# Softmax attention beside a spectral filter: ten score tiles to VectorE and GpSimd, squares to VectorE, a step budget carried from step to step

## The chip, the cores and the metric

The kernel runs on one NeuronCore of a Trainium2 chip. The metric is the device time of one execution in microseconds; less is better. The engines are named as in the profile: PE (TensorE matmuls) and PEld (its weight loads), DVE (VectorE), ACT (ScalarE), POOL (GpSimd), SP (SyncE, which only issues transfers here).

## What is computed

Two branches read the same input `x` (2048 tokens, 448 features) and are mixed per token by a gate.

```python
def reference(A_x, A_wqkv, A_wo, B_x, B_w_r, B_w_i, gate_w):
    # H = 16 heads of Dh = 28, S = 2048, D = 448, all bfloat16
    x = A_x
    g = sigmoid((x * gate_w).sum(-1, keepdims=True))
    q, k, v = split_heads(x @ wqkv)                 # each (1, 16, 2048, 28)
    p = softmax(einsum("bhqd,bhkd->bhqk", q, k) * Dh ** -0.5)
    a = merge_heads(einsum("bhqk,bhkd->bhqd", p, v)) @ wo
    X = rfft2(B_x as float32) * (w_r + 1j * w_i)    # (1, 2048, 225)
    b = irfft2(X, s=(S, D)).astype(bfloat16)
    return g * a + (1 - g) * b
```

## The kernel before

**Attention.** Scores stand transposed: keys on the 128 partitions, queries along the columns. The 16 heads form four groups T of four heads (28 features padded to 32 rows each, so that four heads share the 128 rows), and the 2048 queries form four blocks q of 512. A pair (T, q) is a *chunk*; there are 16. A chunk has 16 key blocks i times 4 heads s, that is 64 *tiles* of 128 x 512 scores, 1024 tiles in all. The tiles, in order, are cut into *steps* of three, 342 steps, so a chunk is 21.33 steps (`SPAN`) and some steps hold tiles of two chunks.

A step m works like this. `scores(m)` makes three matmuls into one three-bank PSUM tile `psS` (two such tiles take turns). `exps(m)` is one ScalarE instruction, `Pt`, which applies exp with the scale to all 1536 columns and writes bfloat16. `values` takes finished tiles in groups of eight (`GROUP`) and makes the value matmuls into `psPV`; a constant one in each head's value block gives the softmax sums in the same matmuls. A constant feature row of the keys, `kb`, and the negated half norms of queries and keys, which `q_units` and `k_units` compute, bound the exponent, so that no maximum over the scores is needed. When a chunk's 64 value matmuls are done, `normalise` transposes `psPV` on VectorE (`turned`, tile `oU`), one step later takes the reciprocal and multiplies on GpSimd (`scaled`, tiles `rc` and `on`), and three steps later transposes back on VectorE (`back`, into `oT`, which is the place of `qT`).

**Background work.** Everything else is cut into *units*: generators that yield the model cost of the next matmul and then issue it. They are the projections (`q_units`, `k_units`, `v_unit`, `first_values`), the spectral branch as matmuls with Fourier matrices (`f1_units`, `stage_A_units`, `f34_units`, `f678_units`), and the output tiles (`out_tile`). All of them use one PSUM bank, `ps_bg`, with one buffer, which VectorE empties at the end of a unit. The spectral weights are multiplied in `f34_units` with half of the products on VectorE and half on GpSimd (tiles `cm_t`, `G`).

`plan` gives each unit a due step; units are kept sorted by it. In each step, after the value matmuls, `other_work` issues pieces of the current unit while the next piece's model cost fits the step's room; when a unit ends, the step's background work ends too. If `scores` needs a projection that is not yet made, `need` runs units without regard to the room until it is. The queries of a chunk c, where T is above 0 or q is above 0, are due from step 21.33 c - 13 to 21.33 c - 8. `filler` adds matmuls on a zero tile, `warm`, ahead of the scores where the model's PE activity of the last steps falls short of a target.

The model's numbers (`ROOM` = 1.22 us for a step's PE work, `SWITCH` = 0.11 us for a change of kind, `MM` = 1/2400 us for a column) set only the order and number of the instructions. Each engine works in the order of the program (`keep_in_program_order`), so whatever stands behind a waiting instruction on its engine waits with it.

**Around it.** `head` runs before step 0: transposes of x, the keys of group 0 and its first query block. `gate`, called in the unit at step 8, computes the gate on ScalarE and VectorE, and `w_copy` copies projection weights on GpSimd. `finish` does the last chunk's normalisation and output.

Of the kernel before, what the change touches and what calls it, by code (L numbers as in the profile page):

```python
# [9 lines left out]
BF16 = mybir.dt.bfloat16  # L10
# [5 lines left out]
P = 128  # L16
# [10 lines left out]
NQ = S // QW  # L27
SCALE = float(DH) ** -0.5
ROOM = 1.22
SWITCH = 0.11  # L30
GROUP = 8
PTB = 6
# [2 lines left out]
FEND = 318  # L35
BUSY = 1650
UNIT = 1000
F = D // 2 + 1
F2 = 2 * F
J = P // NT  # L40
# [94 lines left out]
class Kernel:  # L135
    def __init__(self, tc, A_x, A_wqkv, A_wo, B_w_r, B_w_i, gate_w, out):
        self.tc = tc
        self.nc = Engines(tc)
        self.A_x, self.A_wqkv, self.A_wo = A_x, A_wqkv, A_wo
        self.B_w_r, self.B_w_i, self.gate_w = B_w_r, B_w_i, gate_w  # L140
        assert tuple(A_x.shape) == (1, S, D)
        self.x = A_x[0].rearrange("(p t) d -> p t d", t=NT)
        self.outv = out[0].rearrange("(p t) d -> p t d", t=NT)
        self.units = []
        self.activity = [800, 800]
        self.current = None
        self.later = {}

    def setup_pools(self, ctx):
        tc = self.tc  # L150
# [26 lines left out]
    def loads(self):  # L177
# [13 lines left out]
        self.xtok = [per.tile([P, 4, D], BF16, name=f"xtok{g}", tag=f"xb{g}") for g in range(4)]  # L191
        for g in range(4):
            nc.sync.dma_start(out=self.xtok[g][:], in_=self.x[:, 4 * g:4 * g + 4, :])
        self.kbt = per.tile([P, 1], F32, name="kbt")
        self.kb = self.kbt[:, 0:1]
        wv = self.A_wqkv[:, 2 * D:3 * D].rearrange("(c p) n -> p c n", p=CK)
# [17 lines left out]
        self.wq = self.Wqk[:, :, 0:D].rearrange("p c (h d) -> p c h d", d=DH)  # L214
        self.xT = per.tile([CK, NC_, S], BF16, name="xT")
        self.qT = [per.tile([P, S], BF16, name=f"qT{T}") for T in range(NTH)]
        self.kT = [per.tile([P, S], BF16, name=f"kT{T}") for T in range(NTH)]
        self.oT = self.qT
        self.nm = [per.tile([P, NQ], F32, name=f"nm{T}") for T in range(NTH)]
        self.nhk = [per.tile([P, 1], F32, name=f"nhk{T}") for T in range(NTH)]  # L220
# [139 lines left out]
    def q_units(self, T, g):  # L360
        nc = self.nc
        st = {}

        def a():
            pq = self.ps_bg([P, QW], F32, name="pq")
            yield from self.proj_mm(pq[:], self.WqP, T, g)
            qr = st["qr"] = self.rot3.tile([P, QW], BF16, name="qr")
            nc.vector.tensor_copy(out=qr[:], in_=pq[:])
            sq = st["sq"] = self.rot3.tile([P, QW], BF16, name="sq")
            nc.gpsimd.tensor_tensor(out=sq[:], in0=qr[:], in1=qr[:], op=ALU.mult)  # L370

        def b():
            pq = self.ps_bg([P, QW], F32, name="pq2")
            yield QW * MM
            nc.tensor.matmul(pq[:], lhsT=self.sel, rhs=st["sq"][:], start=True, stop=True)
            nc.vector.scalar_tensor_tensor(out=self.qT[T][:, QW * g:QW * g + QW], in0=pq[:],
                                           scalar=self.nhk[T][:, 0:1], in1=st["qr"][:],
                                           op0=ALU.add, op1=ALU.add)
        return (("qa", T, g), a), (("q", T, g), b)

    def k_units(self, T, g):
        nc = self.nc
        st = {}

        def a():
            pk = self.ps_bg([P, QW], F32, name="pkb")
            yield from self.proj_mm(pk[:], self.WkP, T, g)
            kT = self.kT[T][:, QW * g:QW * g + QW]
            nc.vector.tensor_scalar(out=kT, in0=pk[:], scalar1=self.kb, scalar2=None,
                                    op0=ALU.add)  # L390
            sq = st["sq"] = self.rot3.tile([P, QW], BF16, name="sq")
            nc.gpsimd.tensor_tensor(out=sq[:], in0=kT, in1=kT, op=ALU.mult)

        def b():
            pn = self.ps_bg([P, QW], F32, name="pn")
            yield QW * MM
            nc.tensor.matmul(pn[:], lhsT=self.sel, rhs=st["sq"][:], start=True, stop=True)
            nc.vector.tensor_reduce(out=self.nm[T][:, g:g + 1], in_=pn[:], axis=AX.X, op=ALU.min)
# [98 lines left out]
        return fill  # L497

    def other_work(self, m, room, base=0):
        done = base  # L500
        while self.current is None and self.units and self.units[0][0] <= m:
            self.next_unit()
            self.left = UNIT
        while room > 0 and self.current is not None:
            key, g, cost = self.current
            if cost > room:
                break
            room -= cost
            done += cost / MM
            self.left = max(self.left - cost / MM, cost / MM)  # L510
            try:
                self.current = (key, g, g.send(None))
            except StopIteration:
                self.finished(key)
                break
        self.activity.append(done)

    def need(self, key):
        while key not in self.done:
# [22 lines left out]
    def gate(self):  # L542
# [5 lines left out]
        nc.vector.tensor_scalar(out=self.omg[:], in0=self.gsb[:], scalar1=-1.0, scalar2=1.0,  # L548
                                op0=ALU.mult, op1=ALU.add)

    def attention(self):
        nc = self.nc
        chunks = [(T, q) for T in range(NTH) for q in range(NQ)]
        seq = [(ci, i, s) for ci in range(len(chunks)) for i in range(NT) for s in range(4)]
        steps = [seq[m:m + 3] for m in range(0, len(seq), 3)]
        n = len(steps)
        psS, Pt = {}, {}

        group = [len([1 for k in range(3 * m, 3 * m + 3) if k % GROUP == GROUP - 1])
                 for m in range(n + 1)]  # L560

        def scores(m):
            T, q = chunks[steps[m][-1][0]]
# [8 lines left out]
            for e, (ci, i, s) in enumerate(steps[m]):  # L572
# [12 lines left out]
        self.psPV = None  # L585
        pending = []

        def values(m, least):
            room = 0.0
            while len(pending) >= least:  # L590
                ci = pending[0][2][0]
                T, q = chunks[ci]
                for pt, e, (_, i, s) in pending[:least]:
                    self.need(("v", 1, i) if T else ("v", 0, i // 2))
                    if i == 0 and s == 0:
                        self.psPV = self.ps_pv([P, QW], F32, name="psPV")
                    nc.tensor.matmul(self.psPV[32 * s:32 * s + 32, :],
                                     lhsT=self.vsb[:, i, 4 * T + s, :], rhs=pt[:, e, :],
                                     start=(i == 0), stop=(i == NT - 1), tile_position=(0, 32 * s))
# [3 lines left out]
                if i == NT - 1 and s == 3:  # L603
                    self.normalise(m, T, q, self.psPV)
            return room

        scores(0)
        for m in range(n + 1):
            if m < n:
                exps(m)  # L610
            if m + 1 < n:
                scores(m + 1)
            if m > 0:
                pending += [(Pt[m - 1], e, x) for e, x in enumerate(steps[m - 1])]
# [51 lines left out]
    def normalise(self, m, T, q, psPV):  # L666
# [8 lines left out]
        def scaled():  # L675
# [5 lines left out]
            def back():  # L681
# [239 lines left out]
```

## Time and profile before

| What | Value |
|---|---|
| Median of 3 runs | 501.36 us (499.49, 501.36, 501.70) |
| Profiled execution | 500.02 us, of which the span of its instructions is 498.2 us |
| Mean granted TensorE clock | 0.984 of full speed |
| PE | 407.1 us busy, 82% of the span, 3152 matmuls |
| ACT | 471.6 us busy, 95%, 364 instructions |
| DVE | 195.4 us busy, 39%, 338 instructions |
| POOL | 85.6 us busy, 17%, 125 instructions |
| Steps | the first exponential starts at 17.93 us, the last at 489.2 us |

How to read it: a row of the costliest groups names line, engine, operation, written tile <- read tiles, partitions x elements and type, the count, then the group's busy time, the mean length of one instruction, and the idle time of that engine just before instructions of the group with what ended it. Here nearly all instructions are recorded by one helper, so the line is always L118 and the tiles' names tell them apart. Neighbouring instructions of one engine overlap, so busy time divided by the count is less than the mean length. A timeline row has start, duration, engine, group, count and, in brackets, the idle time before with its releaser.

### The profile page before, as it was taken

The numbers are of one execution on the slowest core, as the hardware profiler recorded it, in microseconds if no ns is written. First come the engines' busy times: TensorE is split into PE (matmuls) and PEld (weight loads), VectorE is DVE, ScalarE is ACT, GpSimd is POOL, SyncE is SP. The second block draws the span as 40 slices with busy tenths as digits, with TensorE's granted clock in tenths as the row PEclk, the third lists the DMA queues.
The fourth block names the chain that finished last, engine by engine and source line by source line (L and its number), as shares of the span: only waits on it lengthen the run. The fifth ranks groups of instructions, "written<-read, shape, count | busy, mean of one in ns | idle before, by whom it ended". The sixth has DMA issues, their size and how long they took to land.

```text
span 498.2 us, 7735 instructions
## 1 busy us (share of the span) xinstructions
PE 407.1 (82%) x3152; PEld 151.9 (30%) x3154; DVE 195.4 (39%) x338; ACT 471.6 (95%) x364; POOL 85.6 (17%) x125
## 2 busy tenths in 40 slices
PE   9777787888888888887887788888888888887886
PEld 5322222222322223323333332332333333322221
DVE  5321222232322325326676773424444333322325
ACT  5899989999999999999989999997999999997993
POOL 4100201040000110003455551001000000000000
PEclk9999989899999999999979999999999999999999
DMA  8700000000000000000122210000000001100002
GB/s 257 184 1 1 2 1 0 1 0 1 2 0 1 0 1 1 0 2 19 42 53 61 52 35 1 1 1 0 22 21 22 22 1 30 51 9 21 18 11 65
DMA packets 15515, 12.67 MB, mean 25 GB/s; under 512 B 6984, under 2 KB 14600, under 8 KB 15480
## 3 DMA queue, kind: packets, MB, share of 16 engines
q1 hardware_dynamic: 14728, 11.91, 8.8%
q8 instruction: 24, 0.39, 0.3%
q10 hardware_dynamic: 752, 0.28, 0.2%
q14 instruction: 11, 0.09, 0.1%
HBM read 10.35 MB, written 1.84 MB: 24 GB/s over the span
## 4 chain that ended last, share of the span: by engine, by line
ACT 54%; issue 20%; PE 17%; DVE 8%; POOL 1%; DVEq 0%; ACTq 0%; POOLq 0%
ACT Pt L118 54%; PE psS L118 5%; PE psPV L118 3%; PE pq L118 2%; PE pvp L118 1%; DVE qT L118 1%; DVE cm_t L118 1%; DVE Xri L118 1%; DVE qr L118 1%; PE psB L118 1%; PE pw L118 1%; PE pt L118 1%; PE pk L118 1%; POOL sq L118 1%; DVE nm L118 1%
## 5 line engine op out<-in xcount | busy, mean ns | idle before, releaser
L118 ACT ACTIVATE Pt<-psS 128x1536 bf16<-128x1536 f32 x342 | 460.2, 1659 | 13.0 <-PE psS L118 12.9
L118 PE MATMUL psS<-qT,kT 32*128 32x512 bf16 x1024 | 136.5, 387 | 31.1 <-ACT Pt L118 22.7
L118 PEld LDWEIGHTS <-kT 32*128 32x128 bf16 x1024 | 47.8, 91 | 148.6 <-issue 140.4
L118 PE MATMUL psPV<-Pt,vsb 128*32 128x512 bf16 x1024 | 80.4, 389 | 0.0
L118 PE MATMUL psS<-warm 128*128 128x512 bf16 (+15 forms) x152 | 43.3, 329 | 23.7 <-ACT Pt L118 20.2
L118 POOL TENSOR_TENSOR sq<-qr 128x512 bf16<-128x512 bf16 x16 | 16.6, 1040 | 162.1 <-DVE qr L118 162.1
L118 POOL TENSOR_TENSOR on<-oU,rc 128x512 bf16<-128x512 f32 x15 | 15.7, 1048 | 101.3 <-DVE rc L118 101.3
L118 POOL TENSOR_TENSOR sq<-kT 128x512 bf16<-128x512 bf16 x12 | 12.5, 1040 | 90.7 <-DVE kT L118 90.7
L118 PEld LDWEIGHTS <-warm 128*128 128x128 bf16 x178 | 17.7, 101 | 27.1 <-issue 23.3
L118 PEld LDWEIGHTS <-vsb 128*32 128x32 bf16 x1024 | 15.6, 94 | 30.0 <-issue 30.0
L118 POOL TENSOR_TENSOR cm_t<-Xri,Wg 128x225 bf16<-128x225 bf16 x32 | 20.2, 654 | 23.1 <-DVE Xri L118 22.9
L118 DVE CAST X<-psx 128x450 bf16<-128x450 f32 x16 | 10.0, 626 | 33.1 <-PE psx L118 33.1
L118 DVE CAST qr<-pq 128x512 bf16<-128x512 f32 x16 | 11.1, 691 | 28.3 <-PE pq L118 28.3
L118 DVE CAST vsb<-pvp 128x336 bf16<-128x336 f32 x16 | 8.1, 508 | 34.6 <-PE pvp L118 34.6
L118 PEld LDWEIGHTS <-xT 112*128 112x128 bf16 x192 | 14.1, 97 | 24.7 <-issue 20.8
L118 DVE TENSOR_SCALAR bm<-psY,omg 128x448 bf16<-128x448 f32 x16 | 10.9, 683 | 27.2 <-PE psY L118 27.2
L118 PE MATMUL pq<-xT,WqP 112*128 112x512 bf16 x64 | 18.9, 382 | 1.3 <-DVE ZT L118 0.3
L118 DVE TENSOR_SCALAR kT<-pkb,kbt 128x512 bf16<-128x512 f32 x12 | 9.0, 751 | 25.5 <-PE pkb L118 25.5
L118 DVE CAST V<-psA 113x512 bf16<-113x512 f32 x16 | 11.1, 691 | 19.7 <-PE psA L118 19.7
L118 DVE CAST U<-psA 113x512 bf16<-113x512 f32 x16 | 11.1, 692 | 19.2 <-PE psA L118 19.1
L118 PE MATMUL psx<-Bd,xT 112*128 112x450 bf16 x64 | 17.0, 356 | 1.7 <-DVE X L118 0.6
L118 PE MATMUL psY<-Binv,ZT 113*128 113x448 bf16 x64 | 16.7, 355 | 1.8 <-DVE fin L118 0.5
(82 smaller groups left out, 359.2 us busy)
## 6 DMA issues: line engine op xcount, KB each, us to landing
RBg<-cRB SPq DMA_DIRECT2D x16, 128.0 KB, 2.1
xtok<-in_A_x_dram SPq DMA_DIRECT2D x4, 448.0 KB, 4.4
out_dram<-fin SPq DMA_DIRECT2D x15, 112.0 KB, 1.7
CSg<-cCS SPq DMA_DIRECT2D x16, 96.0 KB, 1.9
Wg<-in_B_w_r_dram SPq DMA_DIRECT2D x16, 56.2 KB, 1.8
Wg<-in_B_w_i_dram SPq DMA_DIRECT2D x16, 56.2 KB, 1.9
Wqk<-in_A_wqkv_dram SPq DMA_DIRECT2D x1, 784.0 KB, 10.3
Binv<-cBinv SPq DMA_DIRECT2D x1, 448.0 KB, 13.7
```

The costliest lines, as they stand in the source:

```text
L118: return lambda *a, **k: self._tc.keep_in_program_order(f(*a, **k))
```

## The change

Four things are done together.

1. In chunks 0 to 6 and 10 to 12 (`AWAY`), tile i = 0 of head s = 0 is taken out of the ScalarE sequence. It is computed in the chunk's third step, as the third tile of that step's `psS`; the exponential of that step covers two tiles. VectorE multiplies the third tile by scale / ln 2 into float32 (`sx`), and GpSimd raises 2 to that power, elementwise, into bfloat16 (`px`). Its value matmul enters the queue 14 steps later (`LAG`). The start and stop flags of the value matmuls go by a count for each head, and `back` comes 14 steps after the normalisation instead of 3 for head groups 0 to 2.
2. The squares in `q_units` and `k_units` move from GpSimd, where they read the bfloat16 copy twice, to VectorE, where one operand is the PSUM bank and the other the copy.
3. A step's background work may exceed `ROOM` by `ALLOW` = 0.25 us of model time; what it exceeds (`over`) is taken from the steps that follow.
4. The four key tiles `kT` share two buffers, allocated when a group's first key unit runs.

```diff
+ALLOW = 0.25
+LOG2 = SCALE / float(np.log(2.0))
+AWAY = {c: [2] for c in list(range(7)) + [10, 11, 12]}
+LAG = 14
...
+        self.two = per.tile([P, 1], F32, name="two")
+        nc.vector.memset(self.two[:], 2.0)
...
-        self.kT = [per.tile([P, S], BF16, name=f"kT{T}") for T in range(NTH)]
+        self.kT = {}
+        self.new_keys(0)
...
             sq = st["sq"] = self.rot3.tile([P, QW], BF16, name="sq")
-            nc.gpsimd.tensor_tensor(out=sq[:], in0=qr[:], in1=qr[:], op=ALU.mult)
+            nc.vector.scalar_tensor_tensor(out=sq[:], in0=pq[:], scalar=0.0, in1=qr[:],
+                                           op0=ALU.add, op1=ALU.mult)
...
+    def new_keys(self, T):
+        self.kT[T] = self.per.tile([P, S], BF16, name=f"kT{T}", tag=f"kT{T % 2}")
...
-            nc.gpsimd.tensor_tensor(out=sq[:], in0=kT, in1=kT, op=ALU.mult)
+            nc.vector.scalar_tensor_tensor(out=sq[:], in0=pk[:], scalar=self.kb, in1=kT,
+                                           op0=ALU.add, op1=ALU.mult)
...
     def other_work(self, m, room, base=0):
-        done = base
+        done, start = base, room
...
+        return start - room
...
+    def steps(self, chunks):
+        away, acts = {}, []
+        for ci in range(len(chunks)):
+            away[ci] = [(o, (ci, 4 * k, k)) for k, o in enumerate(AWAY.get(ci, []))]
+            out = [x for _, x in away[ci]]
+            acts += [(ci, i, s) for i in range(NT) for s in range(4) if (ci, i, s) not in out]
+        steps, first = [], {}
+        while acts:
+            ci = acts[0][0]
+            m = len(steps)
+            first.setdefault(ci, m)
+            off = [away[ci].pop(0)[1]] if away[ci] and away[ci][0][0] <= m - first[ci] else []
+            k = 3 - len(off)
+            steps.append((acts[:k], off))
+            del acts[:k]
+        return steps
...
             if m > 1:
-                pv = GROUP // 4 * QW * group[m - 2]
-                room = ROOM - 3 * SWITCH - QW * MM - pv * MM
+                pv = GROUP // 4 * QW * group[m - 1]
+                room = ROOM + ALLOW - self.over - 3 * SWITCH - QW * MM - pv * MM
                 self.base += self.filler(m - 1, room, QW + pv, ps)
...
         def exps(m):
-            ne = len(steps[m])
-            pt = Pt[m] = self.rotP.tile([P, 3, QW], BF16, name="Pt")
-            nc.scalar.activation(out=pt[:, 0:ne, :], in_=psS.pop(m)[:, 0:ne, :], func=ACT.Exp,
+            acts, away = steps[m]
+            ne = len(acts)
+            ps = psS.pop(m)
+            pt = self.rotP.tile([P, 3, QW], BF16, name="Pt")
+            nc.scalar.activation(out=pt[:, 0:ne, :], in_=ps[:, 0:ne, :], func=ACT.Exp,
                                  scale=SCALE)
+            ready.setdefault(m + 1, []).extend((pt[:, e, :], x) for e, x in enumerate(acts))
+            for x in away:
+                sx = self.rot2.tile([P, QW], F32, name="sx")
+                nc.vector.tensor_scalar(out=sx[:], in0=ps[:, ne, :], scalar1=LOG2, scalar2=None,
+                                        op0=ALU.mult)
+                px = self.rot2.tile([P, QW], BF16, name="px")
+                nc.gpsimd.tensor_tensor(out=px[:], in0=bcast_last(self.two[:, 0:1], QW),
+                                        in1=sx[:], op=ALU.pow)
+                ready.setdefault(m + LAG, []).append((px[:], x))
...
-                                     start=(i == 0), stop=(i == NT - 1), tile_position=(0, 32 * s))
+                                     start=(count[s] == 0), stop=(count[s] == NT - 1),
+                                     tile_position=(0, 32 * s))
+                    count[s] += 1
...
             fill = self.base - QW
             used = fill * MM + values(m, 4 if late else GROUP)
+            used += 2 * SWITCH + QW * MM
             if m < n:
-                self.other_work(m, ROOM - SWITCH - QW * MM - used - SWITCH, self.base)
+                used += self.other_work(m, ROOM + ALLOW - self.over - used, self.base)
+            self.over = max(0.0, self.over + used - ROOM)
...
-            self.later.setdefault(m + 3, []).append(back)
+            self.later.setdefault(m + (3 if T == NTH - 1 else LAG), []).append(back)
```

More of the change, by code (lines that the diff above doesn't have):

```diff
@@ L147, in __init__ @@
         self.later = {}
+        self.over = 0.0
     def setup_pools(self, ctx):
@@ L385, in a @@
         def a():
+            if g == 0:
+                self.new_keys(T)
             pk = self.ps_bg([P, QW], F32, name="pkb")
@@ L549, in gate @@
                                 op0=ALU.mult, op1=ALU.add)
+    def steps(self, chunks):
[13 more added lines that the diff above has]
+            del acts[:k]
+        assert not any(away.values())
+        return steps
     def attention(self):
@@ L553, in attention @@
         chunks = [(T, q) for T in range(NTH) for q in range(NQ)]
-        seq = [(ci, i, s) for ci in range(len(chunks)) for i in range(NT) for s in range(4)]
-        steps = [seq[m:m + 3] for m in range(0, len(seq), 3)]
+        steps = self.steps(chunks)
         n = len(steps)
-        psS, Pt = {}, {}
-        group = [len([1 for k in range(3 * m, 3 * m + 3) if k % GROUP == GROUP - 1])
-                 for m in range(n + 1)]
+        psS, ready = {}, {}
+        ends = [0]
+        for m in range(n + 1):
+            new = len(steps[m - 1][0]) if m else 0
+            new += sum(1 for k in (m - LAG,) if k >= 0 and steps[k][1])
+            ends.append(ends[-1] + new)
+        group = [ends[m + 1] // GROUP - ends[m] // GROUP for m in range(n + 1)]
         def scores(m):
-            T, q = chunks[steps[m][-1][0]]
+            tiles = steps[m][0] + steps[m][1]
+            T, q = chunks[tiles[len(steps[m][0]) - 1][0]]
             self.need(("k", T, NQ - 1))
@@ L568, in scores @@
             if m > 1:
-                pv = GROUP // 4 * QW * group[m - 2]
-                room = ROOM - 3 * SWITCH - QW * MM - pv * MM
+                pv = GROUP // 4 * QW * group[m - 1]
+                room = ROOM + ALLOW - self.over - 3 * SWITCH - QW * MM - pv * MM
                 self.base += self.filler(m - 1, room, QW + pv, ps)
-            for e, (ci, i, s) in enumerate(steps[m]):
+            for e, (ci, i, s) in enumerate(tiles):
                 T, q = chunks[ci]
@@ L579, in exps @@
         def exps(m):
-            ne = len(steps[m])
-            pt = Pt[m] = self.rotP.tile([P, 3, QW], BF16, name="Pt")
-            nc.scalar.activation(out=pt[:, 0:ne, :], in_=psS.pop(m)[:, 0:ne, :], func=ACT.Exp,
-                                 scale=SCALE)
+            acts, away = steps[m]
[3 more added lines that the diff above has]
+            nc.scalar.activation(out=pt[:, 0:ne, :], in_=ps[:, 0:ne, :], func=ACT.Exp,
+                                 scale=SCALE)
+            ready.setdefault(m + 1, []).extend((pt[:, e, :], x) for e, x in enumerate(acts))
[7 more added lines that the diff above has]
+                ready.setdefault(m + LAG, []).append((px[:], x))
         self.psPV = None
         pending = []
+        count = [0] * 4
         def values(m, least):
@@ L590, in values @@
             while len(pending) >= least:
-                ci = pending[0][2][0]
-                T, q = chunks[ci]
-                for pt, e, (_, i, s) in pending[:least]:
+                for ap, (ci, i, s) in pending[:least]:
+                    T, q = chunks[ci]
                     self.need(("v", 1, i) if T else ("v", 0, i // 2))
-                    if i == 0 and s == 0:
+                    if not any(count):
                         self.psPV = self.ps_pv([P, QW], F32, name="psPV")
                     nc.tensor.matmul(self.psPV[32 * s:32 * s + 32, :],
-                                     lhsT=self.vsb[:, i, 4 * T + s, :], rhs=pt[:, e, :],
-                                     start=(i == 0), stop=(i == NT - 1), tile_position=(0, 32 * s))
+                                     lhsT=self.vsb[:, i, 4 * T + s, :], rhs=ap,
+                                     start=(count[s] == 0), stop=(count[s] == NT - 1),
+                                     tile_position=(0, 32 * s))
+                    count[s] += 1
                 del pending[:least]
@@ L602, in values @@
                 self.base += least // 4 * QW
-                if i == NT - 1 and s == 3:
+                if min(count) == NT:
+                    count[:] = [0] * 4
                     self.normalise(m, T, q, self.psPV)
@@ L612, in attention @@
                 scores(m + 1)
-            if m > 0:
-                pending += [(Pt[m - 1], e, x) for e, x in enumerate(steps[m - 1])]
+            pending += ready.pop(m, [])
             late = m >= n - 3
```

## The prediction

> **What bounds the kernel now.** I read the page first (engines, slices, costliest groups), then the groups with shapes kept apart, ScalarE's timeline, the stretches table, and last PE, VectorE and GpSimd around the places where ScalarE sits idle. The groups with shapes apart give the bound and the prices:
>
> ```profile
> L118 ACT ACTIVATE Pt<-psS 128x1536 bf16<-128x1536 f32 x341 | 459.7, 1661 | 13.0 <-PE psS L118 12.9
> L118 ACT ACTIVATE Pt<-psS 128x512 bf16<-128x512 f32 x1 | 0.8, 841 | 0.0
> L118 DVE SCALAR_TENSOR_TENSOR qT<-pq,nhk,qr 128x512 bf16<-128x512 f32 x15 | 11.2, 749 | 11.3 <-PE pq L118 11.3
> L118 POOL TENSOR_TENSOR on<-oU,rc 128x512 bf16<-128x512 f32 x15 | 15.7, 1048 | 101.3 <-DVE rc L118 101.3
> L118 POOL TENSOR_TENSOR sq<-qr 128x512 bf16<-128x512 bf16 x16 | 16.6, 1040 | 162.1 <-DVE qr L118 162.1
> L118 POOL TENSOR_TENSOR sq<-kT 128x512 bf16<-128x512 bf16 x12 | 12.5, 1040 | 90.7 <-DVE kT L118 90.7
> ```
>
> The exponentials fill 459.7 of the 498.2 us span, one every 459.7/341 = 1.348 us (neighbours overlap, so one lasts 1661 ns). All ScalarE loses between them is 13.0 us, and PE ends nearly all of it. ScalarE's timeline from 103 us on (start, duration, group, count, idle before) shows where:
>
> ```profile
> 104.94 145.19 ACT L118 ACTIVATE Pt<-psS 128x1536 bf16<-128x1536 f32 x108 [0.19 <-PE psS L118]
> ...
> 264.01 75.33 ACT L118 ACTIVATE Pt<-psS 128x1536 bf16<-128x1536 f32 x56 [0.62 <-PE psS L118]
> 342.47 115.63 ACT L118 ACTIVATE Pt<-psS 128x1536 bf16<-128x1536 f32 x86 [3.13 <-PE psS L118]
> 461.27 28.81 ACT L118 ACTIVATE Pt<-psS 128x1536 bf16<-128x1536 f32 x22 [3.16 <-PE psS L118]
> ```
>
> Two holes of 3.13 and 3.16 us make 6.3 of the 13.0. Counting instructions back from the end (22, then 22 + 86), they lie before steps 320 and 234, the steps whose tiles first touch chunks 15 and 11. There `scores` calls `need`: the new chunk's query projection is not done and is forced through. The other 6.7 us are small holes, most beside lowered TensorE clocks in the stretches table (0.94 in 46.7:75.5 and 75.5:104.3, 0.88 in 248.3:277.1).
>
> PE around the first hole:
>
> ```profile
> 338.65 0.69 DVE L118 CAST qr<-pq 128x512 bf16<-128x512 f32 x1 [1.30 <-PE pq L118]
> 339.39 0.60 PE L118 MATMUL psA<-R,G 128*113 128x256 bf16 x4 [0.78 <-DVE qr L118]
> 340.02 0.69 DVE L118 CAST V<-psA 113x512 bf16<-113x512 f32 x1 [0.69 <-PE psA L118]
> 340.77 0.39 PE L118 MATMUL pq<-sq,IS 128*128 128x512 bf16 x1 [0.79 <-DVE V L118]
> ```
>
> The background units share one PSUM bank: the next unit's first matmul waits until VectorE has emptied it (0.78 and 0.79 us).
>
> **The change, part by part.** *Ten tiles off ScalarE.* Per column an exponential costs (1661-841)/1024 = 0.80 ns, so a tile of 512 is 0.41 us. Ten steps carry two exponentials and one moved tile; the other 994 tiles need 332 instructions, 342 together, the number of before. So no instruction is saved, only ten are shortened: 10 x 0.41 = **-4.1 us**. For this to arrive PE must keep up. When PE waits for nothing else it starts the next scores 0.05 us after the exponential that frees the bank, and they take 0.39; so it may be about 1.35-0.05-0.39 = 0.9 us late before ScalarE starves. Subtracting these starts and ends in the timeline, half of the steps are under 0.32 us late and 90% under 0.53; a step shortened by 0.41 still fits. The moved tile's bank is freed by VectorE as well: its multiply (a 512-column read of PSUM, 0.69 to 0.75 us by CAST `qr` and `qT`) can start once the scores stand, about one exponential before ScalarE is done with the bank. Queued behind it on VectorE are background evictions, which would hold PE; charged at nothing, 0.4 us each (4 us) if that cover is gone.
>
> *The power.* No row shows a GpSimd power. From below it is a plain operation on 512 columns, 1.05 us (`on`, float32 input). From above only its consequence is bounded: the value matmul comes 14 steps later, 13 x 1.348 + 0.94 = 18.5 us after the step's start, less 0.75 for the multiply and some 0.7 of hand-overs: about 17 us. Up to 17 us it costs nothing; above, PE, and VectorE in `back` (whose `on` stands behind the power on GpSimd), wait for the excess ten times over. I take the inside, since the nearest row is 1.05 us and the distance to 17 is a factor of 16; the excess stays a rival. The Trainium skill (GPSIMD Engine Reference, section 3.1) states about 12 cycles per element for a data-dependent branch; on 512 elements at its 1.2 GHz that is an estimated 5.1 us for one branch per element, also inside; no run shows it, and the sum would not change.
>
> What speaks against the change stands in the multiplies of the spectral stage:
>
> ```profile
> L118 DVE TENSOR_TENSOR cm_t<-Xri,Wg x32: 280/644/1023, 233.3 to 294.6; 128x225 bf16<-128x225 bf16 x32
> L118 POOL TENSOR_TENSOR cm_t<-Xri,Wg x32: 606/653/670, 233.4 to 295.1; 128x225 bf16<-128x225 bf16 x32
> ```
>
> On VectorE the same multiply takes 280 ns at best (minimum) and 644 in the middle: each pair's second one starts while GpSimd multiplies and ends with it. VectorE operations that read PSUM show no such thing (the transposes `oU` take 702 to 718 ns with GpSimd busy or idle). If a power lay beside one of the 48 VectorE products of this stage (32 `cm_t`, 16 `G`), VectorE would stand for the rest of the power. They run from 233 to 296 us; chunk 6's power starts at step 130 (about 196 us) and chunk 10's at step 215 (about 314), so none meets one if it is under 17 us. The moved squares and the multiply have one input in PSUM: no charge. The Trainium skill (SBUF — State Buffer, "Who interferes with whom") calls this an exclusive lock, which these rows bear out; it adds that a copy or tensor_scalar from SBUF to SBUF may take the lock too. By that page `gate`'s two small VectorE operations at 30.25 us would wait for chunk 0's power, begun near 21.5 us: by it one stall more of 17-8.75 = 8.2 us of VectorE at worst, and nothing for a power under 8.75 us. No row shows a single-input operation held up, so that stall is bounded from below by nothing and from above by the same end of the power; I take 1 us of ScalarE idle: **+1.0**.
>
> *Squares to VectorE.* Of 28 GpSimd squares (1040 ns) 27 move (the head's stays): 27 x 0.75 = 20 us more on VectorE, busy 195.4 of 498.2. The square reads the bank, which is held 0.75 us longer, and PE's wait for it, as above, gets as much longer where it exists. Following the 27 places in the timeline, the extra is 14.0 us of PE waits in all, of which the 0.9 us of slack covers all but 2.5; 2.1 of these fall in the two holes and in a lowered-clock stretch. **+0.5 us**, at most 20 if nothing covered. Waits of PE for GpSimd's squares (3.5 us in three places) shrink, credited at nothing.
>
> *The budget.* A step's model room for background work was 1.22 - 0.11 - 0.213 - 0.11 = 0.787 us, or 0.25 where a value group runs (another 0.11 + 0.427), in three of eight steps. Pieces of 512 columns cost 0.213 and only whole ones fit: 5 x 3 + 3 x 1 = 18 in eight steps. Now a step may overdraw by 0.25 and pays back, so eight steps have 8 x 0.787 - 3 x 0.537 = 4.68 us: 21.9 pieces, 22% more. The backlog against the plan's due steps, from the evictions in VectorE's timeline: 2 steps for the key unit due 106.7 (at 168.4 us), 7 for the one due 192.0 (292.3 us), 12 for the query due 221.7, which is the first hole. Between 106.7 and 192, 85 due steps took 90: a deficit of 5%, which 22% covers. Towards the second hole the units due 285.7 to 307.0 took 29 steps for 21; at 22% more they take 24, and a backlog near 4 grows to 7, with 9 allowed. So both holes go: **-6.3 us**. What is late next is PE behind the busier shared bank, as above, inside its slack; I charge **+0.5**. If the overdraft only brings fillers nearer, the holes stay (next paragraph). The `kT` buffers in pairs, `back` later by 11 steps and the counted starts cost nothing: chunk 3 ends at step 85, the first new key unit is due at 107. No DMA changes.
>
> Sum: -4.1 + 1.0 + 0.5 - 6.3 + 0.5 = -8.4. The profiled execution took 500.02 us (span 498.2 and 1.8 around it): 491.6. The median, 501.36, is 1.3 above it: **493.0 us**. Clock drops are left as they are; they could come or go with about 6.7 us.
>
> **The rivals.** (1) *The power outlasts its lag.* PE, in order, waits at the value matmul and ScalarE behind it. It decides from 17 us; at 22 us it costs 10 x 5 = 50, giving 543. For: nothing in the profile prices a power, and GpSimd's plain operations are already slower than VectorE's. Against: it must be over 16 times the `on` row. Slower. (2) *The holes stay*, the change not doing what its budget says: PE's real limit is the shared bank's emptying, not the model's room. Then -4.1 + 2.0 = -2.1: 499.3, no difference that can be told. For: the 0.78 us waits. Against: PE waits 42.9 us for ScalarE, so it has time. (3) *VectorE late*: held by powers or squares, PE waits longer, its clock drops more often (each drop now shows about 1.6 to 3.3 us of holes): 501 to 506.
>
> **How the numbers follow.** Forecast 0.70 (488 to 498.5); holes stay 0.10; power outlasts 0.12; VectorE late 0.08, half of it within 0.5%. A measurement here tells about 0.5% (2.5 us; the three runs lie 0.4% apart). Faster 0.70, same 0.10 + 0.04 = 0.14, slower 0.12 + 0.04 = 0.16. The range, 487.5 to 505, takes in the clock's 6.7 us below, and the holes and most of a late VectorE above; the power's 0.12 stays outside, with some 0.05 at the ends. The forecast's own range is 488 to 498.5.
>
> **What would show it.** Right: 331 exponentials of 1536 columns, ten of 1024 at near 1250 ns, one of 512; no ScalarE hole over 1 us before steps 234 and 320; GpSimd powers under 17 us and PE never waiting for `px`; VectorE near 222 us busy. Wrong: PE waits on GpSimd `px`, VectorE waits on `on`, or ScalarE idle above 13 us with lowered clocks in more stretches.

## The result, and the profile after

The changed kernel takes 1158.19 us (median of 4 runs, 1151.96 to 1160.95) against 501.53 us: a ratio of 2.3091, 95% interval 2.2966 to 2.3216. The forecast of 493.0 us, with a range to 505, is wrong by a wide margin. The profiled execution took 1160.95 us with a span of 1158.8 us. Some executions of a kernel are over 1.5% longer than its fastest one; the ratios, here and below, leave these out and the medians do not, so the two can differ a little.

The costliest groups of the page, and the exponentials with shapes kept apart (busy time, mean length, idle time before):

```profile
L122 POOL TENSOR_TENSOR px<-two,sx 128x512 bf16<-128x512 f32 x10 | 819.2, 81920 | 10.2 <-DVE sx L122 10.1
L122 PE MATMUL psPV<-px,vsb 128*32 128x512 bf16 x10 | 5.8, 585 | 629.9 <-POOL px L122 629.9
L122 POOL TENSOR_TENSOR on<-oU,rc 128x512 bf16<-128x512 f32 x15 | 15.7, 1048 | 192.8 <-DVE rc L122 192.8
...
L122 ACT ACTIVATE Pt<-psS 128x1536 bf16<-128x1536 f32 x331 | 454.3, 1491 | 666.9 <-PE psS L122 665.5
```

One power of 128 x 512 takes 81.92 us, where an ordinary two-input GpSimd operation of that shape (`on`) takes 1.05. Ten fill 819 us. Their value matmuls are what PE waits for, 629.9 us in ten places, and ScalarE waits for PE's scores behind them. The timelines of GpSimd, PE and ScalarE around the first:

```profile
23.27 81.93 POOL L122 TENSOR_TENSOR px<-two,sx 128x512 bf16<-128x512 f32 x1 [10.14 <-DVE sx L122]
...
40.42 0.40 PE L122 MATMUL psPV<-Pt,vsb 128*32 128x512 bf16 x4
...
105.26 0.58 PE L122 MATMUL psPV<-px,vsb 128*32 128x512 bf16 x1 [64.44 <-POOL px L122]
...
107.04 1.45 ACT L122 ACTIVATE Pt<-psS 128x1536 bf16<-128x1536 f32 x1 [64.31 <-PE psS L122]
```

The value group of eight that holds the moved tile is cut in the middle: four matmuls at 40.42 us, the power's at 105.26. All of PE stands in between, and ScalarE has nothing to do for 64.31 us. Ten such waits, 629.9 us, are 95% of the 660.6 us by which the span grew. Most of the rest lies in shorter holes around them: ScalarE's waits for PE's scores are 667.9 us in all, 38 us more than PE's ten waits, where the kernel before had 12.9; the mean granted TensorE clock is 0.691, against 0.984.

### The profile page after: what moved, and what is told of

It reads as the page before. It is cut to its first block, busy times and chain, and to the rows that moved or that the text cites. A ratio compares the mean times of both kernels' runs of the same rounds, so it can differ in the third digit from the quotient of the medians.

```text
span 1158.8 us, 7784 instructions
## 1 busy us (share of the span) xinstructions
PE 434.5 (37%) x3163; PEld 150.2 (13%) x3163; DVE 220.0 (19%) x376; ACT 475.0 (41%) x364; POOL 876.5 (76%) x108
## 4 chain that ended last, share of the span: by engine, by line
POOL 72%; PE 12%; ACT 8%; issue 4%; DVE 4%; DMA 0%; DVEq 0%; SPq 0%; ACTq 0%; POOLq 0%
POOL px L122 71%; ACT Pt L122 8%; PE psS L122 4%; PE psPV L122 2%; PE psx L122 1%; PE psA L122 1%; PE pkb L122 1%; DVE sq L122 1%; PE pvp L122 1%; POOL on L122 1%; PE pq L122 0%; PE pw L122 0%; DVE kT L122 0%; PE psB L122 0%; DVE Xri L122 0%
## 5 line engine op out<-in xcount | busy, mean ns | idle before, releaser
L122 POOL TENSOR_TENSOR px<-two,sx 128x512 bf16<-128x512 f32 x10 | 819.2, 81920 | 10.2 <-DVE sx L122 10.1
L122 ACT ACTIVATE Pt<-psS 128x1536 bf16<-128x1536 f32 (+1 forms) x342 | 463.6, 1475 | 669.4 <-PE psS L122 667.9
L122 PE MATMUL psPV<-px,vsb 128*32 128x512 bf16 x10 | 5.8, 585 | 629.9 <-POOL px L122 629.9
L122 PE MATMUL psS<-qT,kT 32*128 32x512 bf16 x1024 | 146.8, 420 | 29.5 <-ACT Pt L122 25.5
L122 PE MATMUL psPV<-Pt,vsb 128*32 128x512 bf16 x1014 | 92.2, 423 | 0.4 <-ACT Pt L122 0.3
L122 PEld LDWEIGHTS <-kT 32*128 32x128 bf16 x1024 | 38.4, 92 | 155.1 <-issue 150.7
L122 PE MATMUL psS<-warm 128*128 128x512 bf16 (+18 forms) x161 | 49.0, 364 | 17.4 <-ACT Pt L122 15.8
L122 DVE CAST ZT<-psZ 113x512 bf16<-113x512 f32 x16 | 11.1, 691 | 79.5 <-PE psZ L122 79.4
L122 DVE TENSOR_REDUCE nm<-pn 128x1 f32<-128x512 f32 x16 | 11.0, 690 | 75.8 <-PE pn L122 75.8
L122 PE MATMUL psx<-Bd,xT 112*128 112x450 bf16 x64 | 22.2, 466 | 4.2 <-DVE sq L122 3.0
## 6 DMA issues: line engine op xcount, KB each, us to landing
Binv<-cBinv SPq DMA_DIRECT2D x1, 448.0 KB, 13.1
```

The costliest lines, as they stand in the source:

```text
L122: return lambda *a, **k: self._tc.keep_in_program_order(f(*a, **k))
```

## The experiments

Each ratio is to the kernel before, which lay at 501.9 to 502.5 us (median) in these comparisons.

### The parts, one at a time

*The power replaced by a multiply:* `op=ALU.pow` becomes `op=ALU.mult`, the rest of the change as it is.

> The changed kernel with GpSimd multiplying by two instead of raising two to the power (leaves out the exponential of the ten moved tiles; everything else stays). Theory A, the power's own 81.9 us is the whole loss: the instruction falls to about 1.05 us, no PE wait for px over 1 us, and the time is the forecast's sum without the power's excess, 490 to 496 us. Rival B, the hand-over (VectorE frees the bank late, the value matmul waits in PE's order, back waits for on) costs by itself: 502 us or more, with PE waits for px or sx left.

Measured 507.79 us, ratio 1.0129 (1.0054 to 1.0203). The row of `px` (minimum, median and maximum in ns, then the first and last start):

```profile
L122 POOL TENSOR_TENSOR px<-two,sx x10: 1039/1041/1042, 23.4 to 382.9; 128x512 bf16<-128x512 f32 x10
```

PE no longer waits for it. The power's length is thereby shown as the cause of the great loss: without it 650 us are gone. But theory A's 490 to 496 us is missed as well: the rest of the change is no gain of 8 us, it is a loss of 6, so other terms of the forecast were wrong too. The next three runs take them apart.

*No tile moved:*

```diff
-AWAY = {c: [2] for c in list(range(7)) + [10, 11, 12]}
+AWAY = {}
```

> The changed kernel with no tile moved (squares on VectorE, carried budget, paired key buffers stay). Forecast's sum: 501.5 - 6.3 (holes) + 0.5 + 0.5 = 496 us, no ScalarE hole over 1 us before steps 234 and 320. Rival, the holes stay because PE is limited by the shared bank: 501 to 503 us with holes of some 3 us left.

Measured 503.82 us, ratio 1.0052 (1.0018 to 1.0086), where the forecast's sum was 496. It is not the rival with its holes either: ScalarE's longest wait for scores is 2.0 us. But its waits are 12.2 us in all, as before (12.9), now in 23 places and not 12.

*Budget and key buffers alone:* the same, and the squares again `nc.gpsimd.tensor_tensor` on the copies.

> Budget and key buffers alone (squares back on GpSimd, no tile moved). If the budget closes the two holes: 495.5 us; if the bank is the limit: 501 us. Against the kernel with the squares on VectorE the difference is 0.5 us by the forecast, 5 us or more if the longer hold of the bank reaches ScalarE.

Measured 494.89 us, ratio 0.9855 (0.9804 to 0.9906). ScalarE's timeline from 115 to 482 us:

```profile
114.88 114.34 ACT L122 ACTIVATE Pt<-psS 128x1536 bf16<-128x1536 f32 x85 [0.55 <-PE psS L122]
230.26 1.45 ACT L122 ACTIVATE Pt<-psS 128x1536 bf16<-128x1536 f32 x1 [1.04 <-PE psS L122]
232.11 55.18 ACT L122 ACTIVATE Pt<-psS 128x1536 bf16<-128x1536 f32 x41 [0.41 <-PE psS L122]
287.92 135.82 ACT L122 ACTIVATE Pt<-psS 128x1536 bf16<-128x1536 f32 x101 [0.62 <-PE psS L122]
423.99 57.87 ACT L122 ACTIVATE Pt<-psS 128x1536 bf16<-128x1536 f32 x43 [0.25 <-PE psS L122]
```

From 287.92 us 101 exponentials run without a hole, past step 234, and 43 more, past step 320: the two holes of 3.1 us are gone, and ScalarE waits 6.8 us for scores in all instead of 12.9. That is the budget term of the forecast, and it came in full (-7.3 us; by the interval 5 to 10).

*Squares alone:* the kernel before with only the two `scalar_tensor_tensor` squares.

> The kernel before with only the squares moved to VectorE. Forecast: 502 us (+0.5); if the bank held 0.75 us longer in 27 places is not covered by PE's slack: 506 us or more; if shorter chains of query units count: 500 us.

Measured 509.93 us, ratio 1.0129 (1.0054 to 1.0203): not +0.5 but some +6.5 us. Beside the budget they cost more: 494.89 us without them, 503.82 with them, 9 us. In the waits of the latter, the kernel with no tile moved (who waits for whom: total, times, longest), PE stands behind a square on VectorE 22 times, for 19.6 us, in front of eight of its tiles. Three of them:

```profile
PE psA L122 <- DVE sq L122: 7.3, 9, 1.3
...
PE psB L122 <- DVE sq L122: 2.8, 2, 2.2
PE psx L122 <- DVE sq L122: 2.5, 3, 1.3
```

*Squares on VectorE from the copies in SBUF:* in the kernel before, `nc.gpsimd.tensor_tensor` becomes `nc.vector.tensor_tensor`, with the same operands.

> The kernel before with the 27 squares on VectorE, but both operands the bfloat16 copies in SBUF, so that the shared PSUM bank is free after the first copy as it was. Theory B, what cost 6.5 us (509.9 against 502.2 with the bank as operand) is the longer hold of the bank: back to 500 to 503.5 us. Rival V, VectorE's time itself (its queue delays later evictions): 506 to 510 us.

Measured 500.56 us, ratio 0.9964 (0.9937 to 0.9992). The loss is gone. PE's only waits for these squares are

```profile
PE pq L118 <- DVE sq L118: 1.5, 2, 0.8
```

and all its waits for VectorE are some 29 us, as before (30); in the pair above they are some 25 us without the squares from the bank and 45 with them. So the loss came from the operand: a square that reads the shared PSUM bank keeps it 0.69 to 0.75 us longer, and the next unit stands behind it. From the copies a square is also shorter (0.42 us), so whether VectorE has the time for 27 squares of 0.69 to 0.75 us that hold no bank is not shown.

### What a power costs

In the changed kernel only the last PW columns of each moved tile go to VectorE and GpSimd; ScalarE does the others in an instruction of its own:

```diff
+                nc.scalar.activation(out=px[:, 0:QW - PW], in_=ps[:, ne, 0:QW - PW], func=ACT.Exp,
+                                     scale=SCALE)
+                nc.vector.tensor_scalar(out=sx[:], in0=ps[:, ne, QW - PW:QW], scalar1=LOG2, ...)
+                nc.gpsimd.tensor_tensor(out=px[:, QW - PW:QW],
+                                        in0=bcast_last(self.two[:, 0:1], PW), in1=sx[:], op=ALU.pow)
```

> The changed kernel, but only the last 64 columns of each moved tile go to VectorE and GpSimd's power; ScalarE does the other 448 in an instruction of its own. Theory A, the power costs 160 ns per column (81.92 us / 512) and nothing fixed: 10.2 us each, inside the 17 us that its 14 steps cover, PE waits for px near 0, and the time is that of the kernel with the cheap operation plus ten extra ScalarE instructions of some 0.45 us: 508 to 515 us. Rival F, a large fixed part (a code load or a set-up): the powers stay over 40 us and the time over 700.

> The same with 128 columns. Theory A: 20.5 us each, 3.5 us over the cover of 17 us, so PE waits for px about 3.5 us in each of ten places and the time is about 35 us above the 64-column kernel, 535 to 555 us. If the cover is longer than worked out (18.5 us): +20 us. If the excess is absorbed by PE's slack: no difference.

64 columns: ratio 0.9995 (0.9937 to 1.0053), median 507.42 us, a little under theory A's 508 to 515; why is not shown. 128 columns: 543.04 us, ratio 1.0775 (1.0704 to 1.0845). The power's row of each (minimum, median and maximum in ns, then the first and last start), first for 64, then for 128 columns, and of the waits for 128 columns the one for it (total, times, longest):

```profile
L123 POOL TENSOR_TENSOR px<-two,sx x10: 10522/10523/10537, 22.5 to 383.4; 128x64 bf16<-128x64 f32 x10
```

```profile
L123 POOL TENSOR_TENSOR px<-two,sx x10: 20716/20717/20732, 23.8 to 418.1; 128x128 bf16<-128x128 f32 x10
```

```profile
PE psPV L123 <- POOL px L123: 19.4, 10, 3.0
```

From 64 to 128 columns it is (20.717-10.523)/64 = 0.159 us per column, from 128 to 512 (81.918-20.717)/384 = 0.159 again: a power costs 0.33 us plus 0.159 us per column, and rival F, a large fixed part, falls. With 64 columns PE does not wait for it at all. With 128 it waits 1.9 us on average, so the 14 steps cover 20.7-1.9 = 18.8 us, more than the 17 worked out; the ten waits for the full power say the same (81.9-63.0 = 18.9). The time still rose by 36 us over the 64-column kernel (39 by the ratios), more than the 19.4 us of waits. In the profiled execution ScalarE waits 47.0 us for scores, against 14.3 with 64 columns, and the clock is 0.912, against 0.975; how the two share the rest is not shown.

*A power beside VectorE's two-input products:* moved tiles in chunks 7 to 9 only, 96 columns.

> The changed kernel with moved tiles in chunks 7, 8 and 9 only, the power on 96 columns (15.4 us at 160 ns each), so that it lies beside VectorE's two-input products cm_t and G. If a GpSimd operation that reads SBUF holds VectorE's second input for its whole length: some cm_t or G of VectorE lasts 5 to 15 us and PE and ScalarE stand meanwhile, at most some 13 us in each chunk. If not: cm_t stays at 280 to 1030 ns on VectorE, while GpSimd's own half of the products still waits behind the power.

Measured 517.38 us, once. In VectorE's timeline, with a power on GpSimd from 230.85 to 246.48 us:

```profile
232.54 0.47 DVE L123 TENSOR_TENSOR cm_t<-Xri,Wg 128x225 bf16<-128x225 bf16 x2
233.04 0.28 DVE L123 TENSOR_TENSOR G<-cm_t,cm_t 128x225 bf16<-128x225 bf16 x1
```

Two products take 0.47 us beside the power, and `G` 0.28. In all, 15 of VectorE's products lie inside the three powers, and they take 269 to 351 ns. Nothing stands for the length of the power; VectorE is faster there than beside GpSimd's multiplies. GpSimd's half of the products does wait: it starts at 246.46 us, when the power ends.

### Why ten tiles bring nothing even with a short operation

*Squares on GpSimd and the multiply in place of the power:*

> The changed kernel with a GpSimd multiply in place of the power (leaves out the exponential of the ten moved tiles) and with the squares back on GpSimd. Theory S, the squares on VectorE are what ate the budget's and the tiles' gain, by holding the shared bank and by standing ahead of the moved tile's multiply: 494.9 - 4 + 1 = 490 to 493 us. Rival H, the moved tile itself costs what it saves because VectorE frees psS late: 495 to 500 us.

Measured 495.34 us, ratio 0.9829 (0.9781 to 0.9878): as good as budget alone, and at rival H's lower end. So the squares on VectorE explain the loss, but ten shortened exponentials add nothing that can be seen. The squares also stood in the moved tiles' way, as theory S has it: with them on VectorE the moved tile's multiply comes behind a square in five of the ten places, and ScalarE then starves 0.55 to 1.79 us. The timeline around one moved tile, with the squares on GpSimd:

```profile
143.40 0.69 DVE L122 TENSOR_SCALAR sx<-psS 128x512 f32<-128x512 f32 x1 [0.15 <-ACT Pt L122]
...
144.14 0.41 PE L122 MATMUL psS<-warm 128*128 128x512 bf16 x2 [0.70 <-DVE sx L122]
...
144.98 2.79 ACT L122 ACTIVATE Pt<-psS 128x1536 bf16<-128x1536 f32 x2 [0.28 <-PE psS L122]
```

The multiply waits for the exponential of its own step and ends 0.72 us or more after it, in all ten places. PE waits for it before it may write that `psS` again, 5.0 us in eight places, and here ScalarE then starves 0.28 us. Both read the same tile, in different banks, but the program makes the second reader wait for the first one's semaphore. ScalarE's waits for scores are 8.8 us in this kernel and 6.8 with the budget alone, so 2 of the 4 us are seen to come back as waits; the other 2 are less than these times can tell (each is uncertain by some 2.5 us). Two other orders were tried, both with the squares on GpSimd.

*The multiply ahead of the exponential in program order* (moved up within `exps`, cheap operation), and the same with one VectorE instruction in place of multiply and power, in ten and in 64 tiles:

```diff
+                px = self.rot3.tile([P, QW], I16, name="px")
+                nc.vector.tensor_scalar(out=px[:], in0=ps[:, ne, :], scalar1=128.0 * LOG2,
+                                        scalar2=127 * 128.0 - 7.3, op0=ALU.mult, op1=ALU.add)
+                ready.setdefault(m + LAG, []).append((px[:].bitcast(BF16), x))
```

> The kernel with the squares on GpSimd and the cheap operation (it leaves out the exponential of the ten moved tiles), with VectorE's multiply issued ahead of that step's ScalarE exponential instead of behind it. In the run before, the multiply of all ten tiles ended 0.72 us or more after the exponential, since it waits for ScalarE's semaphore. Theory W, this wait gives the saved 0.41 us back: now the multiply runs while the exponential of the step before runs, and the time falls from 495.3 by 2 to 4 us, to 491 to 493 us. Rival, ScalarE now waits for VectorE in its place or PE is the limit there anyway: 494 to 497 us.

> Carried budget, squares on GpSimd, the same ten tiles, each by one VectorE instruction that scales, shifts and writes a 16-bit integer, whose bits read as bfloat16 are 2 to the power up to a straight line between powers of two (at most some 3% off in these tiles). Issued ahead of the exponential, used two steps later, back after three steps. If VectorE's one instruction (0.69 us) is hidden: 490 to 493 us; if the hand-over costs what it saves: 495 us.

> The same with four tiles in each of the 16 chunks, 64 in all. ScalarE loses 64 x 0.41 = 26 us and VectorE gains 64 x 0.69 = 44 us. If ScalarE stays the bound: 494.9 - 26 = 469 us; with PE's lateness in the shortened steps giving half of it back: 480 us; if PE becomes the bound, its clock drops and holes appear: 490 us or more.

Measured 518.00 us (1.0297, 1.0245 to 1.0348), 518.92 us (1.0312, 1.0266 to 1.0359) and 599.36 us (1.1896, 1.1829 to 1.1962): much worse than the first two expectations, and far above the 490 us of the third's last case. The timeline of the first shows why:

```profile
148.29 0.39 PE L122 MATMUL psS<-qT,kT 32*128 32x512 bf16 x3 [0.41 <-ACT Pt L122]
148.62 0.94 PE L122 MATMUL psx<-Bd,xT 112*128 112x450 bf16 x4
149.60 0.62 DVE L122 CAST X<-psx 128x450 bf16<-128x450 f32 x1 [0.94 <-PE psx L122]
...
150.30 0.63 DVE L122 TENSOR_SCALAR sx<-psS 128x512 f32<-128x512 f32 x1
...
151.04 2.37 ACT L122 ACTIVATE Pt<-psS 128x1024 bf16<-128x1024 f32 x2 [1.46 <-DVE sx L122]
```

The scores stand at 148.68 us, but on VectorE the multiply is queued behind the eviction of the unit that PE does after the scores. It runs at 150.30, and now ScalarE waits 1.46 us for it. Such waits are 13.1 us in nine places here, 14.6 in ten with the one VectorE instruction, and 86.0 in 49 with 64 tiles.

*The multiply issued with the scores*, ahead of that eviction, with ten (cheap operation), 64 and 32 tiles:

```diff
         def scores(m):
...
                                  start=True, stop=True, tile_position=(32 * s, 0))
+            for x in away:
+                ...                # VectorE's operation, then ready
```

> The kernel with the squares on GpSimd and the cheap operation (it leaves out the exponential of the ten moved tiles), with VectorE's multiply issued with the scores, so that on VectorE it stands ahead of the evictions of the step before. Theory Q, VectorE's queue order is what held the bank or ScalarE: the multiply runs right behind the scores, nobody waits for it, and the ten tiles give their 4 us: 490 to 492.5 us against 495.3 with the multiply behind the exponential. Rival, the shortened steps meet PE's limit whatever VectorE does: 494 to 497 us.

> Carried budget, squares on GpSimd, 64 tiles (four in each chunk) by VectorE's one instruction that writes the bits of an approximate power (a straight line between powers of two), issued with the scores. If only the queue order was wrong in the 64-tile kernel at 599 us: ScalarE is the bound, 494.9 - 26 = 469 us, or 480 with half given back in PE lateness. If readers of one psS tile wait for each other anyway or PE is the bound: 495 us or more.

> The same with 32 tiles, two in each chunk at its eighth and fifteenth step, away from the chunk's start where the transposes of the finished chunk stand on VectorE. Saved on ScalarE 32 x 0.41 = 13 us: 482 us if all of it arrives, 488 if half.

Measured 495.06 us (0.9866, 0.9821 to 0.9910), 506.00 us (1.0063, 1.0024 to 1.0101) and 499.48 us (0.9968, 0.9930 to 1.0006). The queue's part is cured, 518 to 495 us, but against the budget alone (494.89 us) nothing is seen to be gained, and more tiles lose more. In the 32-tile kernel:

```profile
116.55 0.60 PE L123 MATMUL psS<-qT,kT 32*128 32x512 bf16 x3
...
117.19 0.69 DVE L123 TENSOR_SCALAR px<-psS 128x512 int16<-128x512 f32 x1 [2.10 <-PE psS L123]
...
117.98 2.37 ACT L123 ACTIVATE Pt<-psS 128x1024 bf16<-128x1024 f32 x2 [0.29 <-DVE px L123]
```

The operation now follows the scores at once, and ScalarE waits for it, since the scores do not stand early enough for 0.69 us more to fit. ScalarE's waits for VectorE's operation, with 10, 32 and 64 tiles:

```profile
ACT Pt L122 <- DVE sx L122: 4.1, 8, 1.0
```

```profile
ACT Pt L123 <- DVE px L123: 13.3, 22, 1.7
```

```profile
ACT Pt L123 <- DVE px L123: 26.3, 42, 2.3
```

The shorter exponentials were to save 4.1, 13 and 26 us: ScalarE waits as long as it saves. So in each order tried one of the two readers pays.

### A version without a second reader

The moved tiles become background units: one score matmul into the shared bank `ps_bg`, the same VectorE instruction, used two steps later. `psS` belongs to ScalarE alone, the steps are full again, and there are fewer of them; `back` comes three steps after the normalisation again.

```diff
+    def moved(self, x):
+        ci, i, s = x
+        T, q = divmod(ci, NQ)
+        ps = self.ps_bg([P, QW], F32, name="psM")
+        yield QW * MM
+        self.nc.tensor.matmul(ps[:], lhsT=self.kT[T][32 * s:32 * s + 32, P * i:P * i + P], ...)
+        px = self.rot3.tile([P, QW], I16, name="px")
+        self.nc.vector.tensor_scalar(out=px[:], in0=ps[:], ...)
+        self.ready.setdefault(self.m + LAG, []).append((px[:].bitcast(BF16), x))
```

> Carried budget and squares on GpSimd, with 32 tiles (two in each chunk) as background units of their own: scores matmul into the shared background bank, one VectorE instruction that writes the bits of an approximate power (a straight line between powers of two), used two steps later; ScalarE's 992 tiles come in 331 full steps. No psS tile has two readers any more. Saved on ScalarE: 11 exponentials of 1.348 us, 14.8 us: 480 us if the readers' order was what ate the gain. Rival, PE and the shared bank are the bound as soon as ScalarE has less: 490 us or more.

> The same with 16 tiles, one in each chunk: 336 steps, 6 exponentials of 1.348 us fewer than before: 487 us if all of it arrives, 492 or more if PE and the shared bank are the bound.

Measured 491.88 us with 32 tiles (0.9815, 0.9751 to 0.9878) and 488.76 us with 16 (0.9742, 0.9682 to 0.9801). With 16 the exponentials are

```profile
L123 ACT ACTIVATE Pt<-psS 128x1536 bf16<-128x1536 f32 x336 | 453.3, 1595 | 7.9 <-PE psS L123 7.3
```

six fewer (five full ones and the short one of 512 columns); idle time before them is 7.9 us, against 6.4 with the budget alone. About 6 of the 8 us arrive (494.89 to 488.76 us, uncertain by some 4), and this is the fastest of all these kernels. With 32 the exponentials' idle time is 15.0 us, 14.2 of it behind PE's scores, and PE's own waits for VectorE are some 44 us, against 33 with 16 tiles and 25 with the budget alone. That is the rival's limit, PE and the shared bank, and it takes more than the further 16 tiles give; how much of it is the lower clock (0.961 against 0.975) is not shown.

## Why the prediction was wrong

**The step that failed** is the power: "I take the inside, since the nearest row is 1.05 us and the distance to 17 is a factor of 16". The power is 78 times the `on` row. Nothing in the profile before priced it, so the distance to the nearest row was no argument, and the 5.1 us estimated there for a branch per element was 16 times too low. The rival that the power outlasts its lag, given 0.12, is what happened, and its mechanism held: PE waits at the value matmul and ScalarE behind it. Its formula gives 493 + 10 x (81.92-17) = 1142 us with the measured power, against 1158.19, but that this is so near is partly luck. The cover was 18.8 us and not 17, and the kernel without the power's length takes 507.79 us and not 493. With the measured parts it is 507.79 + 629.9 = 1138 us; the other 20 us, beside a clock of 0.691, are not taken apart. Why a power costs that much for each column stays open.

One bound was to be had without a price for the power: a chunk is 21.33 steps of 1.348 us, 28.8 us long, and the moved tile must be in before the chunk's sums close. So no later use within the chunk can cover more than that, and a power of 81.92 us is lost with any lag.

**The budget** (-6.3 us) was right in mechanism and size: alone, with the key buffers, it measures 494.89 against 502.16 us, -7.3 us, and both holes are gone. The rival that the holes stay is refuted.

**The squares** (+0.5 us) are mis-sized: alone they cost some 6.5 us (interval 0.54% to 2.03%, 2.7 to 10 us), beside the budget 9. The term took each of 27 PE waits by itself, 14.0 us more in all, and let 0.9 us of slack cover all but 2.5 of them. The mechanism named there, the bank held 0.75 us longer, is right, as the run with the operands in SBUF shows. Beside the budget PE's waits for VectorE grow by some 20 us, and about 9 of them reach the time; that each wait finds the full slack again is not shown by any run, and the measured size speaks against it. How much of the cost is carried-over lateness and how much a clock lowered more often stays open.

**The ten tiles** (-4.1 us) gave nothing that can be told from 0: 495.34 and 495.06 us in two orders, against 494.89 with the budget alone. Failed is the sentence that the multiply "can start once the scores stand, about one exponential before ScalarE is done with the bank": it waits for ScalarE's semaphore, and issued ahead of that it makes ScalarE wait. The working had a price of this size ("0.4 us each (4 us) if that cover is gone") and charged it at nothing.

**What spoke against the change**, a power holding up VectorE's two-input products, does not happen: `cm_t` and `G` take 269 to 351 ns beside a power, near their shortest times. So the +1.0 us for `gate` is wrong as well. Its operation, inside chunk 0's power (23.27 to 105.20 us), took what it took before, 176 ns:

```profile
L122 DVE TENSOR_SCALAR ge<-ge x1: 175/175/175, 30.7 to 30.7; 128x16 f32<-128x16 f32 x1
```

The Trainium skill (SBUF — State Buffer, "Who interferes with whom") calls the ports that the two engines share an exclusive lock, and has a VectorE instruction with two SBUF inputs contend with a GpSimd instruction that reads SBUF. Beside a power, which reads `sx` in SBUF, the two-input products did not wait for its end; nor did this operation, for which that page gives contention only as possible.

**Smaller slips.** ScalarE's holes beside the three lowered-clock stretches add up to 1.4, 1.2 and 2.5 us in its timeline, not to "about 1.6 to 3.3 us" each, and the range's lower end, 487.5, lies 5.5 us under the forecast, so it does not take in the clock's whole 6.7. VectorE's second `cm_t` of a pair ends some 0.13 us after GpSimd's first multiply, not with it. None of these bears on the miss.

## What to carry to other kernels

An operation that no row of the profile shows has no upper price, however cheap its neighbours on that engine are. Set it against the time that its use can be put off, and measure it alone at two sizes before building a pipeline on it. A second engine that reads part of a tile is not free: look for whether the program orders the two readers, and where the new instruction stands in its engine's queue. A shared bank with one buffer is paid for by the length of its last reader, so copy first and work on the copy.

## What the runs showed of the hardware

A GpSimd power with a float32 tensor as exponent cost 0.33 us plus 0.159 us per column on 128 partitions (64 to 512 columns), steady to 16 ns over the ten powers of one width; a multiply on 512 columns cost 1.04 us.

VectorE's two-input product of 128 x 225 took 280 ns beside a GpSimd power, and 644 ns in the middle beside GpSimd multiplies in the kernel before. What the two engines contend for is thus not held for the length of a power.
